# Two slices of an input weight loaded together, in 4,096-byte rows

## The chip, the cores and the metric

The kernel runs on one core of a Trainium2 chip. The metric is the device time of one execution in microseconds; the time of the kernel before is the median of three executions. Where the text works inside an execution, it uses one profiled execution, with times counted from the start of its span.

## What is computed

Cosformer attention (8 batches, 8 heads, 576 positions, 64 features a head) is followed by a two-layer feed-forward block with a swish whose slope is learned per hidden feature.

```python
# attention, q, k, v: (8, 8, 576, 64)
q_p, k_p = phi(q, cos_w, sin_w), phi(k, cos_w, sin_w)   # [relu(x)*cos, relu(x)*sin]
kv = np.einsum('bhsf,bhsd->bhfd', k_p, v)
z = np.sum(k_p, axis=2)
num = np.einsum('bhsf,bhfd->bhsd', q_p, kv)
den = np.einsum('bhsf,bhf->bhs', q_p, z)[..., None] + 1e-06
x = (num / den).transpose(0, 2, 1, 3).reshape(4608, 512)
# feed-forward, w_in: (512, 2048), w_out: (2048, 512), beta: (2048,)
h = x @ w_in
g = h * (1.0 / (1.0 + np.exp(-beta * h)))
out = g @ w_out
```

## The kernel before

The 4,608 tokens are nine chunks of 512. For each chunk TensorE computes h in 16 tiles of 128 hidden features (512 deep, so four matmuls a tile, numbered mi = 0 to 3), ScalarE applies Silu with beta as scale, and TensorE multiplies by w_out. Chunks 0 and 1 do this with plain matmuls (L384 for h; L542 for the output of chunk 0); the later ones use a Strassen-like scheme. Attention of batch b is woven in between, so that x of the next chunk is ready in time. The program order of each engine is the order in which the code is written: nothing reorders it, and an instruction that waits holds all behind it on its engine.

Both weights come from HBM in float32 and are cast to bfloat16 in SBUF. w_in is loaded in four slices of 512 of the 2,048 hidden features. Slice i goes into one staging buffer of 128 partitions x 4 x 512 float32 (there are four such buffers), one request for each mi, each of 128 rows of 2,048 bytes (L101). Because x comes transposed in an order of its own, partition 2d + jj of the buffer at place mi = 2 jp + g holds row 256 jp + 128 jj + 64 g + d of w_in; in HBM neighbouring rows lie 8,192 bytes apart. `cast_win` (L106) then writes `win[i]` in bfloat16. For slices 1, 2 and 3 this is `cast_halves` (L752): two casts on VectorE, each over all four mi and one half of the 512 columns. Slice i feeds h's tiles 4i to 4i + 3.

The four parts of w_out (`load_w("out", 0)` to `3`) take the same four staging buffers again, each as soon as the casts that read it are done.

All these loads are issued by SP's queue, in this order: q, v and k of batch 0, slice 0 of w_in (L135), slices 1 to 3 (L722), then in `rest()` w_out 0 and 1, then raw_v, raw_k and raw_q of batch 1 (L765 to L767, one 1,152 KB request each, recorded as L79), then w_out 2 and 3 in halves. Each request has one of eight completion semaphores, taken in turn, and SP waits before an issue until the request eight before it has landed.

VectorE's order around the change is: casts of slice 1; in `rest()` casts of slices 2 and 3; a division step for the last block of batch 0 (L306, L310, L317); eight casts of w_out (L122); the scaling of raw_v of batch 1 (L217); relu of raw_k (L191); relu of raw_q (L191).

TensorE's order is: h tiles 0 to 4 of chunk 0, a few matmuls of attention, then (`rest()` stands here) h tiles 5 to 15 without a break, then the output matmuls of chunk 0 (L542). Between these it does `kv_mm` of batch 1 (L274, needs the relu of raw_k) at place 22 of the loop over 32 places, and at place 23, in `second()`, the transposes of q of batch 1 (L233), which need the relu of raw_q.

Of the kernel before, what the change touches and what calls it, by code (L numbers as in the profile page):

```python
# [22 lines left out]
def kernel(  # L23
# [14 lines left out]
    nc = tc.nc  # L38
# [37 lines left out]
    def load_raw(b, name, j0=0, j1=4):  # L76
        js = slice(j0, j1)
        src = {"q": q, "k": k, "v": v}[name][b]
        nc.sync.dma_start(  # L79
            out=raw_tile(b, name)[:, js].rearrange("q j n d -> q j (n d)"),  # L80
            in_=src.rearrange("(j g) (p n) d -> (g p) j (n d)", g=2, n=NQ)[:, js, :])

    win = [const.tile([P, MI, 512], BF16, name=f"win{i}") for i in range(4)]
# [7 lines left out]
    w_in_v = moe_w_in.rearrange("(jp jj g d) f -> jp g d jj f", jp=2, jj=2, g=2)  # L91
    w_out_v = moe_w_out.rearrange("(j p) m -> p j m", p=P)
    stages = {}

    def load_w(kind, i, step=4):
        if (kind, i) not in stages:
            stages[kind, i] = stage.tile([P, 4, 512], FP32, name="w_stage", tag="w_stage")
        st = stages[kind, i]
        if kind == "in":
            for mi in range(MI):  # L100
                nc.sync.dma_start(out=st[:, mi], in_=w_in_v[mi // 2, mi % 2, :, :, i * 512 : (i + 1) * 512])  # L101
            return
        for a in range(0, 4, step):
            nc.sync.dma_start(out=st[:, a : a + step], in_=w_out_v[:, 4 * i + a : 4 * i + a + step, :])

    def cast_win(i, mis, eng="dve", f0=0, f1=512):  # L106

        o, a = win[i][:, mis, f0:f1], stages["in", i][:, mis, f0:f1]
        if eng == "act":
            nc.scalar.copy(o, a)  # L110
        elif eng == "pool":
            nc.gpsimd.tensor_copy(o, a)
        else:
            nc.vector.tensor_copy(o, a)

    def cast_out(j, eng="d"):
        i, jj = divmod(j, 4)
        st = stages["out", i]
        if eng == "a":
            nc.scalar.activation(wout[:, j, :], st[:, jj, :], AF.Copy, scale=rbeta[:, j : j + 1])  # L120
        else:
            nc.vector.tensor_scalar(wout[:, j, :], st[:, jj, :],  # L122
                                    scalar1=rbeta[:, j : j + 1], scalar2=None, op0=ALU.mult)
# [9 lines left out]
    load_raw(0, "k", 2, 3)  # L133
    load_raw(0, "k", 3, 4)
    load_w("in", 0, 2)  # L135


# [55 lines left out]
    def q_relu(b, jp, eng="dve", n0=0, n1=NQ):  # L193
        return relu(qb[:, jp, n0:n1].rearrange("q n (j d) -> q j n d", j=2),
                    raw_tile(b, "q")[:, 2 * jp : 2 * jp + 2, n0:n1], eng)

    def k_relu(b, j0=0, j1=4, eng="dve", n0=0, n1=NQ):
        relu(rk.rearrange("q n j d -> q j n d")[:, j0:j1, n0:n1], raw_tile(b, "k")[:, j0:j1, n0:n1], eng)

    def v_scale(b, cs, jp=None, n0=0, n1=NQ, eng="dve"):  # L200
        t = (cos9, sin9)[cs]
        rv = raw_tile(b, "v")
        js = slice(0, 4) if jp is None else slice(2 * jp, 2 * jp + 2)
        if jp is not None and eng != "act":
            if eng == "dve":
                t = ps[:, 0, 16 * cs : 16 * cs + NQ]
            (nc.gpsimd if eng == "pool" else nc.vector).tensor_tensor(
                vb[:, n0:n1, js, cs, 0:D],
                rv.rearrange("q j n d -> q n j d")[:, n0:n1, js],
                t[:, n0:n1].unsqueeze(2).unsqueeze(3).to_broadcast([P, n1 - n0, 2, D]), op=ALU.mult)  # L210
            return
        for n in range(n0, n1):
            o, a = vb[:, n, js, cs, 0:D], rv[:, js, n, :]
            if eng == "act":
                got = nc.scalar.activation(o, a, AF.Copy, scale=t[:, n : n + 1])  # L215
            else:
                got = nc.vector.tensor_scalar(o, a, scalar1=t[:, n : n + 1], scalar2=None, op0=ALU.mult)  # L217
        return got
# [82 lines left out]
    def x_rden(bank, slot, n0, n1, jps):  # L301

        w, m = len(jps), n1 - n0
        nv = ps[:, bank : bank + 2, slot * E : (slot + w * m) * E].rearrange("q j (i s e) -> q j i s e", s=w, e=E)
        den = small.tile([P, 2, m, w], FP32, name="den", tag=f"den{m}{w}")
        nc.vector.tensor_tensor(  # L306
            den, nv[:, :, :, :, D],
            eps9[:, n0:n1].unsqueeze(1).unsqueeze(3).to_broadcast([P, 2, m, w]), op=ALU.add)
        rden = small.tile([P, 2, m, w], FP32, name="rden", tag=f"rden{m}{w}")
        nc.vector.reciprocal(rden, den)  # L310
        return nv, rden, n0, jps

    def x_mul(got, n0, n1):
        nv, rden, first, jps = got
        a, z, w = n0 - first, n1 - first, len(jps)
        o = xs[:, n0:n1, jps[0] : jps[-1] + 1].rearrange("q n s (d j) -> q j n s d", j=2)
        nc.vector.tensor_tensor(  # L317
            o.rearrange("q j n s d -> q j (n s) d"),
            nv[:, :, a:z, :, 0:D].rearrange("q j n s d -> q j (n s) d"),
            rden[:, :, a:z].rearrange("q j n s -> q j (n s)").unsqueeze(3).to_broadcast([P, 2, (z - a) * w, D]),  # L320
            op=ALU.mult)
# [41 lines left out]
    def x_turn_dma(b, n0, n1):  # L363
        for c, o, n0, n1 in pieces(b, n0, n1):
            nc.sync.dma_start(out=xt_tile(c)[:, o : o + n1 - n0].rearrange("q n s c -> q (n s) c"),
                              in_=xs[:, n0:n1].rearrange("q n s c -> q (n s c)"), transpose=True)
# [354 lines left out]
    for i in range(1, 4):  # L721
        load_w("in", i)  # L722
# [17 lines left out]
    for mi, eng in enumerate(("pool", "dve", "act", "pool")):  # L740
        cast_win(0, slice(mi, mi + 1), eng)
# [10 lines left out]
    def cast_halves(i):  # L752
        for f in (0, 256):
            cast_win(i, slice(0, MI), "dve", f, f + 256)
# [2 lines left out]

    def rest():

        cast_halves(2)  # L760
        cast_halves(3)
        x_mul(x_rden(2, 0, 8, NQ, (0, 1)), 8, NQ)
        load_w("out", 0)
        load_w("out", 1)
        load_raw(1, "v")  # L765
        load_raw(1, "k")
        load_raw(1, "q")  # L767
        load_w("out", 2, 2)
        load_w("out", 3, 2)
        x_turn_dma(0, 8, 9)  # L770
        for j in range(8):
            cast_out(j)
        v_scale(1, 0)
        v_scale(1, 1, n0=8)
        k_relu(1, 0, 2)
        q_relu(1, 0)
        q_relu(1, 1, n1=5)
# [8 lines left out]
    def second():  # L786
# [14 lines left out]

    early = {
        4: lambda: (num_mm(0, 8, 0, 2, 0), num_mm(0, 8, 1, 2, 1), rest()),
        15: lambda: (v_scale(1, 1, n1=8, eng="act"), k_relu(1, 2, 4, "act")),
        22: lambda: (kv_mm(1, 0, 6), kv_mm(1, 1, 6), kv_take((0, 1), 6, "act"), q_relu(1, 1, "act", 5)),
# [281 lines left out]
```

## Time and profile before

| what | value |
|---|---|
| median of three executions | 276.92 us (275.34, 276.92, 278.1) |
| the profiled execution's own time | 277.77 us |
| its span in the profile | 275.6 us |
| TensorE matmuls (PE) busy | 265.4 us, 96% of the span |
| TensorE weight loads (PEld) busy | 206.8 us, 75% |
| VectorE (DVE) busy | 218.9 us, 79% |
| ScalarE (ACT) busy | 188.6 us, 68% |
| GpSimd (POOL) busy | 62.8 us, 23% |
| moved by the DMA engines | 54.00 MB in 50,856 packets |
| hardware queue of SP (q1) | 47,680 packets, 45.56 MB, 60.7% of 16 engines' span |
| w_in requests | 16 of 256 KB, 5.5 us from issue to landing (median) |
| w_out requests | 2 of 1,024 KB, 9.5 us, and 4 of 512 KB, 12.1 us |

Engines are named as in the profile: PE and PEld are TensorE's matmuls and weight loads, DVE is VectorE, ACT is ScalarE, POOL is GpSimd, SP issues most transfers; SPq is its queue. A line such as L384 is a line of the kernel and can be one in a helper. Idle time of an engine carries the name of what ended it. A request runs on all 16 DMA engines; each engine works its own share off in order and reports once, and the request has landed with the sixteenth report. Times of instructions come from one execution; matmuls are pipelined and their ends are modelled.

### The profile page before, as it was taken

What the parts mean: (1) busy time and instruction counts of PE and PEld (TensorE: products, weight loads), DVE (VectorE), ACT (ScalarE), POOL (GpSimd) and SP (SyncE); (2) the same over time, 40 slices, a digit from 0 to 9 for tenths busy, and PEclk for the clock granted to TensorE, in tenths of its full rate; (3) what the DMA queues carried; (4) which work ended last, traced back from release to release, by engine and by line L of the source; (5) the groups of instructions that cost most, each with busy time, mean ns of one, the idle gap of its engine ahead of it and who ended that gap; (6) DMA issues with size and microseconds to landing.
All of it is one profiled execution on the core that took longest, in us unless ns stands there. A gap on an engine that the chain in (4) does not pass through costs nothing.

```text
span 275.6 us, 8960 instructions
## 1 busy us (share of the span) xinstructions
PE 265.4 (96%) x3712; PEld 206.8 (75%) x3712; DVE 218.9 (79%) x581; ACT 188.6 (68%) x384; POOL 62.8 (23%) x82
## 2 busy tenths in 40 slices
PE   8789998999899999999999999999999999999994
PEld 8444445545784578888888888878888888888883
DVE  5875559499989989899988997898589868758852
ACT  5678778697418647799579966987696169428910
POOL 1320000330059100560075009400840060000000
PEclk9999999999999999999999999999999999999999
DMA  6999999999998998994499658973600560015005
GB/s 231 380 347 336 397 390 289 392 227 321 298 133 289 293 345 167 248 358 100 102 227 354 135 59 207 337 75 59 172 11 2 61 177 8 2 26 128 0 2 152
DMA packets 50856, 54.00 MB, mean 196 GB/s; under 512 B 31408, under 2 KB 31936, under 8 KB 50816
## 3 DMA queue, kind: packets, MB, share of 16 engines
q1 hardware_dynamic: 47680, 45.56, 60.7%
q0 software_dynamic: 2784, 7.61, 9.5%
q8 instruction: 29, 0.48, 0.8%
q10 hardware_dynamic: 352, 0.27, 0.4%
q14 instruction: 11, 0.09, 0.2%
HBM read 36.71 MB, written 9.44 MB: 167 GB/s over the span
## 4 chain that ended last, share of the span: by engine, by line
PE 86%; DMA 9%; DVE 1%; issue 1%; SPq 1%; ACT 0%
PE ps L619 31%; PE ps L509 27%; PE ps L384 12%; DMA raw_q<-in_q_dram 6%; PE ps L561 4%; PE ps L295 4%; DMA raw_v<-in_v_dram 4%; PE ps L274 3%; PE ps L542 3%; SPq L79 1%; PE ps L354 1%; PE ps L233 0%; DVE xs L317 0%; DVE qb L191 0%; DVE rden L310 0%
## 5 line engine op out<-in xcount | busy, mean ns | idle before, releaser
L535 POOL DMA_DIRECT2D out_dram<-o_sb x58 | 33.4, 582 | 157.9 <-ACT o_sb L656 87.2
L418 ACT ACTIVATE g_t<-ps,beta 128x512 bf16<-128x512 f32 x96 | 60.4, 704 | 1.4 <-PE ps L509 1.3
L619 PEld LDWEIGHTS <-S 128*128 128x128 bf16 x448 | 43.4, 98 | 5.2
L509 PE MATMUL ps<-w_stage 128*128 128x256 bf16 x288 | 46.6, 272 | 0.0
L384 PE MATMUL ps<-xt,win 128*128 128x512 bf16 (+1 forms) x196 | 42.8, 375 | 0.0
L509 PEld LDWEIGHTS <-w_stage 128*128 128x128 bf16 x384 | 37.3, 98 | 4.9
L392 ACT ACTIVATE g_t<-ps,beta 128x512 bf16<-128x512 f32 x48 | 32.3, 689 | 7.2 <-PE ps L384 7.1
L485 DVE TENSOR_TENSOR ps<-ps,p 128x256 f32<-128x256 f32 x74 | 30.5, 428 | 8.4 <-PE ps L509 2.9
L619 PEld LDWEIGHTS <-g_t 128*128 128x128 bf16 x336 | 32.3, 98 | 4.5 <-ACT g_t L418 0.4
L384 PEld LDWEIGHTS <-win 128*128 128x128 bf16 x196 | 18.7, 98 | 20.9
L509 PE MATMUL ps<-xt,win 128*128 128x256 bf16 x192 | 32.9, 272 | 0.0
L509 PEld LDWEIGHTS <-win 128*128 128x128 bf16 x288 | 28.0, 98 | 3.5
L619 PE MATMUL ps<-wout,g_t 128*128 128x256 bf16 x224 | 28.9, 273 | 0.0
L478 ACT COPY ps<-ps 128x256 f32<-128x256 f32 x62 | 22.6, 384 | 8.2 <-PE ps L619 4.8
L404 DVE TENSOR_TENSOR S<-g_t 128x512 bf16<-128x512 bf16 (+1 forms) x66 | 25.7, 419 | 3.0 <-ACT g_t L418 1.9
L215 ACT ACTIVATE vb<-raw_v,sin 128x256 bf16<-128x256 f32 (+1 forms) x58 | 26.1, 506 | 2.6 <-DMA raw_v<-in_v_dram 2.6
L619 PE MATMUL ps<-T,S 128*128 128x256 bf16 x224 | 26.6, 273 | 0.0
L619 PE MATMUL ps<-wout,S 128*128 128x256 bf16 x224 | 26.4, 273 | 0.0
L317 DVE TENSOR_TENSOR xs<-ps,rden 128x768 bf16<-128x768 f32 (+4 forms) x26 | 24.3, 941 | 0.9 <-DVE rden L310 0.2
L217 DVE TENSOR_SCALAR vb<-raw_v,cos 128x256 bf16<-128x256 f32 x63 | 19.9, 365 | 1.3 <-DMA raw_v<-in_v_dram 1.3
L221 POOL TENSOR_TENSOR qs<-qt,tanr 128x1152 bf16<-128x1152 bf16 x6 | 14.3, 2390 | 28.1 <-DMA qt<-qb 21.5
L656 ACT COPY o_sb<-ps 128x512 f32<-128x512 f32 x11 | 6.3, 587 | 20.1 <-PE ps L619 20.1
(112 smaller groups left out, 399.4 us busy)
## 6 DMA issues: line engine op xcount, KB each, us to landing
raw_v<-in_v_dram SPq DMA_DIRECT2D x7, 1152.0 KB, 10.3
raw_k<-in_k_dram SPq DMA_DIRECT2D x7, 1152.0 KB, 9.8
raw_q<-in_q_dram SPq DMA_DIRECT2D x7, 1152.0 KB, 7.5
out_dram<-o_sb POOLq DMA_DIRECT2D x58, 128.0 KB, 4.7
w_stage<-in_moe_w_in_dram SPq DMA_DIRECT2D x16, 256.0 KB, 5.5
w_stage<-in_moe_w_out_dram SPq DMA_DIRECT2D x2, 1024.0 KB, 9.5
w_stage<-in_moe_w_out_dram SPq DMA_DIRECT2D x4, 512.0 KB, 12.1
out_dram<-o_sb SPq DMA_DIRECT2D x10, 128.0 KB, 2.3
```

The costliest lines, as they stand in the source:

```text
L215: got = nc.scalar.activation(o, a, AF.Copy, scale=t[:, n : n + 1])
L217: got = nc.vector.tensor_scalar(o, a, scalar1=t[:, n : n + 1], scalar2=None, op0=ALU.mult)
L317: nc.vector.tensor_tensor(o.rearrange("q j n s d -> q j (n s) d"), nv[:, :, a:z, :, 0:D].rearrange("q j n s d -> q j (n s) d"), rden[:, :, ...
L384: nc.tensor.matmul(ps[:, h_bank(c, jt), i * 64 : (i + w) * 64], lhsT=win[jt // 4][:, mi, (jt % 4) * P : (jt % 4 + 1) * P], rhs=xt[:, i : i ...
L392: return nc.scalar.activation(gs[c, jt // 4][:, jt % 4], ps[:, h_bank(c, jt)], AF.Silu, scale=beta[:, jt : jt + 1])
L404: return nc.vector.tensor_tensor(o, l, r, op=op)
L418: return nc.scalar.activation(gs[c, jt // 4][:, jt % 4], bank, AF.Silu, scale=beta[:, jt : jt + 1])
L478: return nc.scalar.copy(at("a", 0), at("b", 0))
L485: nc.vector.tensor_tensor(dst, at("b", 0), st["p5"], op=ALU.add)
L509: nc.tensor.matmul(dst, lhsT=l[:, g], rhs=r[:, :, g * HP : (g + 1) * HP], start=start and g == 0, stop=g == 1, skip_group_check=True)
L535: (eng or own).dma_start(out=out_v[bb, n][:, m0:m1], in_=o_sb[hf * HP : (hf + 1) * HP, m0:m1])
L619: nc.tensor.matmul(dst, lhsT=l(i), rhs=r[:, i], start=start and i == 0, stop=i == order[-1], skip_group_check=True)
```

## The change

Slices 0 and 1 of w_in are loaded as before. Slices 2 and 3, which are columns 1,024 to 2,047, are loaded together: instead of four requests for each slice, one for each mi with rows of 2,048 bytes, there are four requests in all, one for each (jp, g), each of 128 rows of 4,096 bytes that span both slices. The staging buffer that held slice 2 now holds jp = 0 of both slices, and the one that held slice 3 holds jp = 1 of both. The casts of these slices are cut differently to match: each still covers 128 x 1,024 elements, but two mi and all 512 columns, in place of all four mi and 256 columns. So each slice needs both staging buffers. Their order is slice 2 jp 0, slice 2 jp 1, slice 3 jp 0, slice 3 jp 1.

```diff
@@ load_w
-        if kind == "in":
+        if kind == "in" and i < 2:
             for mi in range(MI):
                 nc.sync.dma_start(out=st[:, mi], in_=w_in_v[mi // 2, mi % 2, :, :, i * 512 : (i + 1) * 512])
             return
+        if kind == "in":
+            for g in range(2):
+                nc.sync.dma_start(out=st[:, 2 * g : 2 * g + 2].rearrange("q a f -> q (a f)"),
+                                  in_=w_in_v[i - 2, g, :, :, 1024:2048])
+            return
@@ cast_win
-        o, a = win[i][:, mis, f0:f1], stages["in", i][:, mis, f0:f1]
+        o = win[i][:, mis, f0:f1]
+        if i < 2:
+            a = stages["in", i][:, mis, f0:f1]
+        else:
+            a = stages["in", 2 + mis.start // 2].rearrange("q (g u) f -> q g u f", g=2)[:, :, i - 2, f0:f1]
@@ rest
-        cast_halves(2)
-        cast_halves(3)
+        for i in (2, 3):
+            for jp in range(2):
+                cast_win(i, slice(2 * jp, 2 * jp + 2))
```

## The prediction

> **What bounds the kernel now.** I read the page first, for the chain of work that ended last (shares of the span by engine).
>
> ```profile
> PE 86%; DMA 9%; DVE 1%; issue 1%; SPq 1%; ACT 0%
> ```
>
> TensorE sets the end, and transfers own a tenth of it. The chain in order of time (start, us, what), for 20 to 44 us, shows where that tenth touches this change:
>
> ```profile
> 23.36 2.30 PE ps L384 x11
> 25.65 15.69 DMA raw_q<-in_q_dram
> 41.35 0.03 issue
> 41.37 0.77 DVE qb L191
> 42.14 0.05 issue
> 42.19 1.18 PE ps L233 x18
> ```
>
> The reader is to see that TensorE's work at 42.19 us hangs on the landing of raw_q of batch 1, a transfer that stands behind all of w_in in SP's queue. Then the waits of PE (us in total, times, longest), for 12 to 60 us:
>
> ```profile
> PE ps L233 <- DVE qb L191: 0.7, 1, 0.7
> ...
> PE ps L274 <- DVE rk L191: 0.4, 2, 0.2
> ```
>
> and for 43 us to the end:
>
> ```profile
> PE ps L295 <- issue: 1.5, 2, 0.9
> ```
>
> So all that a faster queue can give TensorE is 0.70 us before L233 and, by the timeline of PE, 0.18 us before the L274 of batch 1 (39.18 us): 0.88 us. After 43 us no transfer and no engine holds TensorE, so what it gains or loses at 42.19 us reaches the end whole. Next the timeline of DVE, where the casts stand (start, us, idle before and its releaser):
>
> ```profile
> 22.98 1.29 DVE L114 CAST win<-w_stage 128x1024 bf16<-128x1024 f32 x2 [1.62 <-DMA w_stage<-in_moe_w_in_dram]
> 25.69 1.29 DVE L114 CAST win<-w_stage 128x1024 bf16<-128x1024 f32 x2 [1.41 <-DMA w_stage<-in_moe_w_in_dram]
> ...
> 29.68 1.68 DVE L122 TENSOR_SCALAR wout<-w_stage,rbeta 128x512 bf16<-128x512 f32 x4 [1.93 <-DMA w_stage<-in_moe_w_out_dram]
> ```
>
> The casts wait for transfers, not for DVE. Last, busy time by stretch (its last two figures are the DMA engines' share and GB/s) and SP's own timeline:
>
> ```profile
> 20.00:26.00 6.00, 6.00 (x49) 3.07 (x47) 2.90 (x5) 5.09 (x9) 0.00 (x0) 1.00 0.98 328
> 26.00:34.00 8.00, 8.00 (x39) 3.63 (x37) 5.02 (x13) 6.19 (x9) 0.00 (x0) 1.00 1.04 387
> 34.00:42.00 8.00, 7.31 (x100) 3.43 (x97) 4.11 (x13) 5.57 (x11) 0.00 (x0) 1.00 1.05 390
> ```
>
> ```profile
> 18.00 2.99 SPq L101 DMA_DIRECT2D w_stage<-in_moe_w_in_dram  x4
> 21.18 1.01 SPq L104 DMA_DIRECT2D w_stage<-in_moe_w_out_dram  x2
> 22.23 0.72 SPq L79 DMA_DIRECT2D raw_v<-in_v_dram  x1
> ```
>
> The DMA engines are saturated up to 42 us; the stretch with w_in moves 328 GB/s where the later ones move 390. A request counts as landed when the slowest of its 16 engines is done, and in the trace's landing events that engine trails the first by 1.4 to 2.9 us. Its work is what counts, and in these events it is busy nearly throughout: from the first request of slice 2 on, each 256 KB lands 0.65 us after the one before.
>
> **The change part by part.** *Rows.* Slices 2 and 3 are 8 requests of 128 rows of 2,048 bytes: 64 packets on each engine. They become 32 packets of 4,096. In the trace's packet records a 2,048-byte packet takes 84 ns (median), a 1,024-byte one 46, a 2,304-byte one 93; SP's queue has none of 4,096, but GpSimd's output queue does, at 159 ns. From 1,024 to 2,048 bytes costs 38 ns, so 4,096 would be 84 + 2 x 38 = 160 ns: both rows agree on 8 to 9 ns saved a pair, 32 x 8 = 0.26 us. The other end: by landing steps the 2,304-byte rows go at 94 ns a packet, 24.5 bytes/ns, against 81.5 ns (25.1 bytes/ns) for 2,048, so longer rows need not be better; at 24.5 bytes/ns 4,096 takes 167 ns against 163, a loss of 32 x 4 = 0.13 us. I take 0.26, since one of its rows has the very size.
>
> [...] The trace's rows decide for me: 256 bytes take 18 ns and 1,024 take 46, so 9 ns of every packet are fixed.
>
> *Fewer requests.* Four completion packets fewer on each engine, 9 ns each by the packet records: 0.04 us. Four issues fewer on SP, some 0.54 us each plus waits (the smallest and median of L101's durations are 534 and 536 ns). A request waits for the landing of the one eight before it, which is why SP sends one every 0.65 us from 13 to 20 us. With twice the bytes in a request, w_out's first request leaves at about 18.3 us (when the casts of slice 0 are done) instead of 21.18. That buys nothing on the slowest engine where it is not starved: w_out 0 was issued at 21.18 and landed at 29.65. What might be starvation: one step of 0.93 and one of 0.74 us among the 0.65s (0.37 over), and w_out 0 taking 4.08 us where w_out 1 takes 2.66; of those 1.42 us, 0.955 are one packet of queue 8, instruction loading, that begins at 25.10, which leaves 0.47 unexplained. Bounds 0 to 0.84; I take 0, because each of these requests had been issued 3 to 8 us before it landed.
>
> *Casts.* Four of 128x1024 before and after, at 694 and 685 ns; source and target keep two free dimensions, so 0 (10 ns either way). What changes is who needs what. Before, tile 8 of h (the first of slice 2) needed DVE's first cast of slice 2, ended at 23.68, and its matmuls began at 25.89. Now its third matmul needs the second cast, which waits for the last w_in request of all. That landed at 25.57 before; 0.12 to DVE's start and 0.69 for the cast give 26.38, and with the 98 ns weight load about 26.5, against 26.32 where that matmul began: a new wait of 0.2 us on TensorE if the queue gains nothing, none if it gains 0.2 or more. Behind it in TensorE's order stand all of h's tiles 9 to 15 and ScalarE's Silus. Its cover is the 0.88 us that TensorE waits later; without that it would cost its 0.2. Tiles 12 to 15 need slice 3's casts at 29.34; they end near 27, 2 us early. On DVE behind the casts stand 0.8 us of work at L306 to L317, and then 1.93 us idle, which hides a cast that ends 0.2 us later.
>
> *Staging buffers* come free after the third and fourth cast instead of the second and fourth: w_out 2 takes the first of them, and SP reached it at 28.98, over 2 us after that.
>
> *Sum.* The queue lands 0.26 + 0.04 = 0.30 us earlier from slice 3 on (bounds -0.13 and 0.29 + 0.04 + 0.84 = 1.17). raw_q lands at 41.05, TensorE's turn begins at 41.89, and the end moves by 0.30 us, as 0.30 is under 0.88 and over 0.2. What is late next is raw_q still.
>
> **The rivals.** *The whole wait goes (B).* If the 328 GB/s was starvation and 4 KB rows cure it, the queue gains about 1 us, and TensorE's 0.88 us close entirely: 276.0 us. For it: the low rate, and the long steps. Against it: the slowest engine's even 0.65 us steps. It can't give more, as TensorE has nothing else to win.
>
> *Hidden or not done (C).* The packets stay at the old bytes per ns, or are cut at 2,048 bytes again: gain 0 to 0.04 us, the new 0.2 us wait falls in the later one: 276.9.
>
> *Long rows are slow (D), the slower side.* The trace's longest packets do move worse: 8,192 bytes take 423 ns (median of 18), 16,384 take 1,085 (of 29), and of the 4,096-byte packets one in ten takes over 350. At 423/2 = 211 ns the 32 packets cost 32 x (211 - 163) = 1.5 us; slice 3, raw_q and the turn come 1.5 us later, and tile 8 waits inside that: 278.5. At 1,085/4 = 271 ns it is 3.5 us, 280.4. It is over 1% from 163 + 2,800/32 = 250 ns a packet on. Against it: those long packets are instruction and table loads on other queues, and the undisturbed 4,096-byte packet takes 159.
>
> **How the numbers follow.** The profiled execution took 277.77 us (span 275.6), 0.85 over the median 276.92; in it I expect 277.47, and as a median 276.92 - 0.30 = 276.6. Chances: forecast 0.50, B 0.17, C 0.15, D 0.18. One per cent is 2.8 us, and it is also the spread of the three runs (275.34 to 278.1), about what a measurement can tell from no change. None of the forecast, B and C leaves it by itself. With the spread of runs on top of B and the forecast I give faster 0.09; half of D's cases reach it with the spread: slower 0.10; within 0.81. Range: from 275.3 (B with the run spread) to 278.5 (D by the 8,192-byte row), with some 0.07 left out below and 0.10 above.
>
> **What would show it.** Right: the DMA packets of queue 1 fall by 512 data packets and 64 completions; the last w_in lands near 25.3, raw_q near 41.05; PE's wait before L274 at 39 us goes, the one before L233 shrinks from 0.70 to about 0.6 us (41.31 to 41.89), and none appears at L384. B: that wait is gone and the rate in 20 to 26 us is near 390. C: raw_q at 41.3 and some 0.2 us of wait at L384. D: casts of slice 2 in two halves far apart, a long wait at L384 near 26.3 us, and L233 after 43 us. The forecast is wrong if the end moves by other than raw_q's landing.

## The result and the profile after

Twenty runs of each kernel: 276.96 us before (median, 274.73 to 278.46), 275.55 us after (274.0 to 279.69). The ratio is 0.995 with a 95% interval of 0.9925 to 0.9974, a gain of 0.7 to 2.1 us. Two later comparisons with fresh runs gave 0.9964 [0.9931, 0.9997] and 0.9988 [0.9951, 1.0025]; the mean of the three, weighted by the inverse square of the intervals' widths, is 0.996 plus or minus 0.002, some 1.0 us (0.5 to 1.5). The profiled execution took 274.12 us with a span of 272.0, so it was 1.4 us under its median, as that of before was 0.8 us over its own: the 3.65 us between the two are not the change's effect alone. The profile of the first repetition, further down, is of a slow execution (278.23 us), and nothing rests on its times.

The page of the changed kernel, its chain by engine:

```profile
PE 89%; DMA 8%; issue 0%; DVE 0%; SPq 0%; DVEq 0%
```

The same chain in order of time, from 20 to 44 us:

```profile
16.12 8.56 DMA w_stage<-in_moe_w_in_dram
...
24.78 0.71 DVE win L123
25.49 0.05 issue
25.53 6.65 PE ps L393 x30
32.18 0.86 PE ps L551 x4
...
38.23 1.15 PE ps L283 x72
39.37 0.16 issue
39.53 0.81 PE ps L551 x3
40.34 1.00 PE ps L242 x18
```

Before, the chain ran through the landing of raw_q to the transposes of q (L233, now L242). Now it runs through the last w_in request and the second cast (L123) to TensorE's tile 8 (L393), and from there it is TensorE's work almost to the end. The waits of PE, 12 to 60 us, say the same: the one before the transposes is gone, a small one at L393 is new.

```profile
PE ps L304 <- ACT kv L293: 0.5, 1, 0.5
PE ps L393 <- DVE win L123: 0.3, 1, 0.3
PE ps L283 <- DVE rk L200: 0.2, 1, 0.2
PE ps L551 <- issue: 0.2, 1, 0.2
```

VectorE's timeline. The first cast stands alone, since the second needs the other staging buffer; w_out 0 (L131) is now there before VectorE asks:

```profile
22.22 0.69 DVE L123 CAST win<-w_stage 128x1024 bf16<-128x1024 f32 x1 [1.23 <-DMA w_stage<-in_moe_w_in_dram]
24.78 1.90 DVE L123 CAST win<-w_stage 128x1024 bf16<-128x1024 f32 x3 [1.87 <-DMA w_stage<-in_moe_w_in_dram]
...
27.42 1.68 DVE L131 TENSOR_SCALAR wout<-w_stage,rbeta 128x512 bf16<-128x512 f32 x4
```

And busy time by stretch, with the DMA engines' rate at the end:

```profile
20.00:26.00 6.00, 5.67 (x42) 2.35 (x41) 2.90 (x6) 4.97 (x8) 0.00 (x0) 1.00 1.03 401
26.00:34.00 8.00, 7.95 (x38) 3.64 (x38) 5.57 (x17) 6.31 (x10) 0.00 (x0) 1.00 1.05 390
```

401 GB/s from 20 to 26 us, where before it was 328. Queue 1 has 47,104 packets in place of 47,680, 576 fewer, as 512 data packets and 64 completions make. The trace's packet records give 159 ns (median) for the 512 packets of 4,096 bytes.

Not all of raw_q's lead belongs to the change. The profile of before ran late ahead of anything that was changed: its first w_in request landed at 15.37 us, in the changed kernel's at 14.06. So more profiles of both were needed, and the experiments gave them.

### The profile page after: what moved, and what is told of

It is laid out like the page before. It is cut to its first block, busy times and chain, and to the rows that moved or that the text cites. A ratio compares the mean times of both kernels' runs of the same rounds, so it can differ in the third digit from the quotient of the medians.

```text
span 272.0 us, 8950 instructions
## 1 busy us (share of the span) xinstructions
PE 264.6 (97%) x3708; PEld 206.7 (76%) x3712; DVE 218.2 (80%) x581; ACT 188.3 (69%) x384; POOL 62.8 (23%) x82
## 3 DMA queue, kind: packets, MB, share of 16 engines
q1 hardware_dynamic: 47104, 45.56, 60.7%
## 4 chain that ended last, share of the span: by engine, by line
PE 89%; DMA 8%; issue 0%; DVE 0%; SPq 0%; DVEq 0%
PE ps L628 32%; PE ps L518 27%; PE ps L393 13%; DMA w_stage<-in_moe_w_in_dram 6%; PE ps L551 5%; PE ps L570 5%; PE ps L304 4%; PE ps L283 3%; DMA raw_v<-in_v_dram 2%; PE ps L242 0%; SPq L79 0%; PE ps L363 0%; DVE win L123 0%; DVE o_sb L659 0%; DVEq L123 0%
## 5 line engine op out<-in xcount | busy, mean ns | idle before, releaser
L393 PE MATMUL ps<-xt,win 128*128 128x512 bf16 (+1 forms) x196 | 43.0, 375 | 0.4 <-DVE win L123 0.3
L393 PEld LDWEIGHTS <-win 128*128 128x128 bf16 x196 | 18.7, 98 | 21.6 <-DVE win L123 0.8
```

What stands on the lines that cost most here:

```text
L393: nc.tensor.matmul(ps[:, h_bank(c, jt), i * 64 : (i + w) * 64], lhsT=win[jt // 4][:, mi, (jt % 4) * P : (jt % 4 + 1) * P], rhs=xt[:, i : i ...
```

## The experiments

Two theories stood against each other. *Supply*: in the kernel before, the faster of the 16 DMA engines run out of work, as at most eight requests are in flight and each is small; larger requests cure it. *Rows*: longer rows do it. A third had to be excluded, that the first pair of profiles differed by chance.

**The kernel before once more.**

> The kernel before once more, for a second profile of it. All theories: 277.0 us within 0.3%. In the first profile the DMA engines moved 328 GB/s from 20 to 26 us and the first w_in request landed at 15.4 us; in the profile of the changed kernel it landed at 14.1 us, ahead of anything that the change touches. If that lead of 1.3 us is a difference between executions, this profile should show a landing somewhere between 13.5 and 15.5 us, and a wait of TensorE before the transposes of q (0.7 us in the first profile) that is not the same as there. The low rate from slice 1 of w_in on should be there again (320 to 350 GB/s) if it belongs to the kernel.

Ratio 0.9992 [0.9959, 1.0026]. Its second w_in request landed at 14.89 us, in the first profile at 16.04 and in the changed kernel's at 14.74, so the early lead is a difference between executions. The low rate and the wait are there again (stretch, then TensorE's timeline):

```profile
20.00:26.00 6.00, 6.00 (x45) 2.77 (x43) 1.99 (x4) 5.22 (x9) 0.00 (x0) 1.00 1.00 316
```

```profile
40.84 1.18 PE L233 MATMUL ps<-ident,qb 128*128 128x128 bf16 x18 [0.71 <-DVE qb L191]
```

**The changed kernel, twice more.**

> The changed kernel once more: ratio 0.995 within 0.003 (275.6 us). Supply theory (with at most eight requests in flight, requests of 256 KB leave the faster DMA engines without work, larger ones do not): the rate while slices 2 and 3 and w_out 0 move is 385 GB/s or more again, and TensorE does not wait before the transposes of q. If the first profile was a lucky execution: the rate is again near 330 and the wait is back.

> The changed kernel once more, beside the others of this call: ratio 0.995 to 0.9965; in the profile, turn of q between 39.9 and 41.2 us with no wait or a short one before it.

Ratios 0.9964 [0.9931, 0.9997] and 0.9988 [0.9951, 1.0025]. In the profile of the second repetition the rate from 20 to 26 us was 397 GB/s, and no wait stood before the transposes of q (waits of PE, 12 to 60 us):

```profile
PE ps L304 <- issue: 1.9, 1, 1.9
PE ps L304 <- ACT kv L293: 0.5, 1, 0.5
PE ps L393 <- DVE win L123: 0.2, 1, 0.2
```

The new wait at tile 8 was 0.2 us here. The first repetition's profile had 403 GB/s and no wait before the transposes either, but 1.47 us at tile 8. The reader also sees why one profile can't weigh a gain of 1 us: a single "issue" wait of TensorE, for which the profile shows no releaser, took 1.9 us here and 0.5 in the first profile of the changed kernel.

**Rows alone, first try.** Rows of 4,096 bytes, eight requests of 256 KB, each of 64 neighbouring partitions:

```diff
-                nc.sync.dma_start(out=st[:, 2 * g : 2 * g + 2].rearrange("q a f -> q (a f)"),
-                                  in_=w_in_v[i - 2, g, :, :, 1024:2048])
+                for u in range(2):
+                    nc.sync.dma_start(out=st[u * 64 : (u + 1) * 64, 2 * g : 2 * g + 2].rearrange("q a f -> q (a f)"),
+                                      in_=w_in_v[i - 2, g, u * 32 : (u + 1) * 32, :, 1024:2048])
```

> The changed kernel with its four 512 KB requests cut into eight of 256 KB, each 64 partitions of 4,096-byte rows: the rows of the change with the request count and bytes in flight of before. Row theory (longer rows move faster): like the changed kernel, 275.6 us, rate 385 GB/s or more. Supply theory: like the kernel before, 277.0 us, rate about 330 while slices 2 and 3 move, and SP again waits for a landing before each of these requests.

Neither: 282.67 us, ratio 1.0209 [1.0162, 1.0257]. The 4,096-byte packets took 256 to 270 ns from 19 to 24 us (means by the us), where the change's took 160 to 162, and the rate fell to 255 GB/s. TensorE's timeline, 20 to 32 us, shows where that went:

```profile
22.14 1.04 PE L394 MATMUL ps<-xt,win 128*128 128x512 bf16 x4 [0.64 <-DVE win L124]
...
30.59 1.80 PE L394 MATMUL ps<-xt,win 128*128 128x512 bf16 x5 [3.96 <-DVE win L124]
```

The run says nothing on rows; it shows that requests for 64 neighbouring partitions were slow here. No run shows why.

**Rows alone, second try.** The same eight requests, but each for every second partition:

```diff
-                nc.sync.dma_start(out=st[:, 2 * g : 2 * g + 2].rearrange("q a f -> q (a f)"),
-                                  in_=w_in_v[i - 2, g, :, :, 1024:2048])
+                for jj in range(2):
+                    nc.sync.dma_start(out=st[jj::2, 2 * g : 2 * g + 2].rearrange("q a f -> q (a f)"),
+                                      in_=w_in_v[i - 2, g, :, jj, 1024:2048])
```

> The changed kernel with eight requests of 256 KB in place of four of 512, rows still 4,096 bytes, each request for every second partition so that it covers both halves of the partitions (the run with 64 neighbouring partitions had packets of 256 ns). Descriptor theory (before, DMA engines wait for descriptors once their backlog is used up, some 150 to 165 rows a us over all engines; a longer row brings more bytes with each): like the changed kernel, ratio 0.995 to 0.998, 4,096-byte packets at 160 ns mean, 385 GB/s or more from 20 to 26 us, no wait before the transposes of q. Request theory (the number of requests is what counts): like the kernel before, ratio 1.000, rate 320 to 340. If it is again the half of the partitions that a request covers: packets well over 160 ns and over 1.01.

Ratio 1.001 [0.997, 1.005], the request theory's number. But the profile is half way: 358 GB/s from 20 to 26 us (packets of 160 to 188 ns, means by the us from 19 to 23 us), and no wait before the transposes of q, only 0.31 us at tile 8.

```profile
20.00:26.00 6.00, 5.69 (x43) 2.51 (x42) 2.10 (x4) 5.06 (x8) 0.00 (x0) 1.00 1.00 358
```

**Requests alone, twice.** The kernel before with two mi in one request, rows of 2,048 bytes, casts as before (added lines only):

```diff
@@ load_w
+        if kind == "in" and i >= 2:
+            for jp in range(2):
+                nc.sync.dma_start(out=st[:, 2 * jp : 2 * jp + 2],
+                                  in_=w_in_v[jp, :, :, :, i * 512 : (i + 1) * 512].rearrange("g d jj f -> d jj g f"))
+            return
```

> The kernel before with slices 2 and 3 loaded in two requests of 512 KB each, still in rows of 2,048 bytes (two mi in one request), casts as before. Supply theory: like the changed kernel or better, 275.3 to 275.6 us, rate 385 GB/s or more, and no wait at the first tile of slice 2, since its cast needs no later slice. Row theory: like the kernel before, 277.0 us, rate about 330.

> Rows of 2,048 bytes in requests of 512 KB once more, beside the change: in the first comparison it was 0.9993 [0.9965, 1.0021] while the change was 0.9964. If requests alone do it: 0.996. If both longer rows and larger requests are needed: 0.999 to 1.000, with a wait before the transposes of q of 0.7 us again and a low rate (under 350 GB/s) from 16 us until the w_in packets are gone.

Ratios 0.9993 [0.9965, 1.0021] and 1.000 [0.9967, 1.0034]: no gain. From 16 to 20 us the rate was 300 and 315 GB/s, from 20 to 26 us 354 and 334. TensorE's timeline of the first, 36 to 43 us, has both late waits:

```profile
39.18 1.33 PE L279 MATMUL ps<-vb,rk 64*64 64x130 bf16 x72 [1.03 <-DVE rk L196]
40.43 1.04 PE L547 MATMUL ps<-wout,g_t 128*128 128x512 bf16 x4
42.18 1.01 PE L238 MATMUL ps<-ident,qb 128*128 128x128 bf16 x15 [0.71 <-DVE qb L196]
```

**Half the row length.** If the DMA engines waited for row descriptors, rows of 1,024 bytes would be a disaster. Eight requests of 256 KB with 256 rows each (of the added lines, those that differ from the edit above):

```diff
@@ load_w
+            for jp in range(2):
+                for f in (0, 256):
+                    nc.sync.dma_start(out=st[:, 2 * jp : 2 * jp + 2, f : f + 256],
+                                      in_=w_in_v[jp, :, :, :, i * 512 + f : i * 512 + f + 256].rearrange("g d jj f -> d jj g f"))
```

> The kernel before with slices 2 and 3 in eight requests of 256 KB whose rows are 1,024 bytes (two mi and half the columns in one request), so the same requests and bytes with twice the rows. Descriptor theory: at 150 to 200 rows a us these 2,048 rows take 10 to 13 us in place of some 5.6, the rate there falls to 160 to 200 GB/s, TensorE waits 4 us or more at h tiles 8 to 12, and the time is 280 to 284 us, ratio 1.013 to 1.03. Packet theory (each packet has a fixed cost of 9 ns and nothing else): 128 packets of 46 ns in place of 64 of 84, 0.5 us later, ratio 1.000 to 1.003.

Ratio 1.0006 [0.9969, 1.0042]; the descriptor theory falls. The engines took 324 to 346 of these packets a us from 18 to 22 us, about twice what that theory allowed, at 342 to 356 GB/s. The rate from 20 to 26 us is even above the 328 and 316 of the kernel before, and the time is no better:

```profile
20.00:26.00 6.00, 6.00 (x45) 2.72 (x43) 2.46 (x4) 5.24 (x9) 0.00 (x0) 1.00 1.07 358
```

**The cut of the casts alone.** The diff is the change's last hunk.

> The kernel before with only the cut of the casts changed (two mi and all 512 columns in one cast, loads as before). All theories: the casts take 0.69 us as before and the first tile of slice 2 needs both casts, which end near 24.3 us, 2 us before that tile; ratio 1.000 within 0.003. If it came out below 0.997, the cut of the casts would have a part in the gain.

Ratio 1.0015 [0.9979, 1.0051]: no part in the gain. Its profile had the wait before the transposes (0.44 us) and another one behind it, at L542 for a cast of w_out:

```profile
40.25 1.18 PE L233 MATMUL ps<-ident,qb 128*128 128x128 bf16 x18 [0.44 <-DVE qb L191]
...
42.07 1.89 PE L542 MATMUL ps<-wout,g_t 128*128 128x512 bf16 x8 [0.64 <-DVE wout L122]
```

**Is raw_q what sets TensorE's turn?** The changed kernel with 1 MB of unneeded loads ahead of raw_q:

```diff
         load_raw(1, "k")
+        for t, j in ((T1, 0), (T2, 2)):
+            nc.sync.dma_start(out=t.rearrange("q i t -> q (i t)").bitcast(FP32).rearrange("q (j m) -> q j m", j=2),
+                              in_=w_out_v[:, j : j + 2, :])
         load_raw(1, "q")
```

> The changed kernel with 1 MB of loads that nobody needs put ahead of raw_q of batch 1 (2.7 us of the queue at 390 GB/s; w_out 2 and 3 come later by as much). Theory that the landing of raw_q sets TensorE's turn and that nothing after it gives time back: TensorE waits some 2.5 us before the transposes of q, they begin near 42.6 us instead of 39.9 to 41.2, and the time grows by 2.4 to 2.8 us over the change: ratio to the kernel before 1.004 to 1.007. If TensorE had slack there, less: 0.996.

Ratio 1.0083 [1.0049, 1.0117], 278.56 us, and the wait is back (TensorE's timeline):

```profile
42.99 1.28 PE L242 MATMUL ps<-ident,qb 128*128 128x128 bf16 x18 [2.48 <-DVE qb L200]
```

Against the change's 0.996 that is about 3.4 us (2.3 to 4.4 by the two intervals), against the changed kernel's median in the same comparison (275.54 us) 3.0. The wait of 2.48 us is not given back. That the loss is more than the wait lies within the interval; a reason for more, a granted clock of 0.50 for 3.4 us, is told in the last section.

**What can a faster queue give at most?** The kernel before without the loads of slice 3:

```diff
@@ load_w
+        if (kind, i) == ("in", 3):
+            return
@@ cast_win
-        o, a = win[i][:, mis, f0:f1], stages["in", i][:, mis, f0:f1]
+        o, a = win[i][:, mis, f0:f1], stages["in", min(i, 2)][:, mis, f0:f1]
```

> The kernel before without the loads of slice 3 of w_in (its casts read slice 2's staging buffer, so the output is not the reference's): everything behind it in SP's queue lands some 2.6 us earlier. It shows what a faster queue could give at most here. Theory: raw_q is there before TensorE asks, no wait at L233 and none at tile 8, and TensorE gains the whole of its later waits, 0.7 to 0.9 us and no more: ratio 0.995 to 0.9975, the same as the change's. If the queue holds TensorE elsewhere too: 0.990 or less.

Ratio 0.9953 [0.9921, 0.9984], with no wait at tile 8 nor before the transposes. TensorE was busy without a break from 20 to 42 us; the last stretch of that, where the kernel before has 7.31 us in 8.00:

```profile
34.00:42.00 8.00, 8.00 (x119) 4.55 (x117) 4.96 (x13) 5.66 (x12) 0.00 (x0) 1.00 1.05 386
```

So leaving a whole megabyte out gains 1.3 us (0.4 to 2.2), about as much as the change does: with raw_q there in time, TensorE has no wait for it left to lose. The queue itself gained less than the 2.6 us expected: relu of raw_q began at 39.39 us, where the two profiles of the kernel before have 41.37 and 40.03.

**Taking the new wait away.** The change with the 128 columns of tile 8 cast first:

```diff
-        for i in (2, 3):
-            for jp in range(2):
-                cast_win(i, slice(2 * jp, 2 * jp + 2))
+        cast_win(2, slice(0, 2))
+        for f0, f1 in ((0, 128), (128, 512)):
+            cast_win(2, slice(2, 4), "dve", f0, f1)
+        for jp in range(2):
+            cast_win(3, slice(2 * jp, 2 * jp + 2))
```

> The changed kernel with the cast of slice 2, jp 1, cut once more, so that the 128 columns of the first tile are cast first (256 elements a partition, some 0.27 us in place of 0.69). In two profiles of the changed kernel TensorE waited 0.3 and 1.5 us at L393 for that cast. Theory that this new wait now sets the end: TensorE starts that tile 0.4 us earlier wherever it waits, ratio to the kernel before 0.993 to 0.996, a little under the change's 0.995 to 0.996. If the wait is covered later: same as the change.

Ratio 0.9959 [0.9925, 0.9994]. TensorE ran through tile 8 without a wait and began the transposes at 39.90 us without one:

```profile
22.84 4.48 PE L393 MATMUL ps<-xt,win 128*128 128x512 bf16 x20
```

The wait is gone, but the intervals can't tell this kernel from the change.

## Why the prediction was right in direction and too small in size

*What bounds the kernel: right.* All five profiles with the loads of before or with larger requests or shorter rows have 0.70 to 0.71 us of wait before the transposes of q, the one with only the casts cut has 0.44; the change's, the split casts, the ceiling and the second try with rows have none. The cap of 0.88 us, worked out from one profile, holds within the ceiling's interval. It is one execution's: the second profile of the kernel before has no wait for raw_k at 38 us and so 0.71 in all, while three variants waited 0.32, 0.41 and 1.03 us for raw_k alone. And "after 43 us no transfer holds TensorE" was true of that execution, but the cast kernel's waited 0.64 us for w_out at 42 us.

*Rows: the packet right, the saving too large.* 160 ns forecast, 159 measured. But what counts by the prediction's own words is the engine that lands last. There a 512 KB request landed 1.28 us after the one before (20.84, 22.12 in the landing events) where two of 256 KB took 1.31. That is 0.03 us a request and some 0.13 for all four, completions included, where the forecast had 0.30. The prediction's landing steps, 163 ns for a pair of packets against 160, had pointed to the smaller saving; it went by the packets' medians. By those (2 x 84 - 159 = 9 ns a pair) the 32 pairs would save an estimated 0.29 us, over twice what the landing steps show with the completions.

*Starvation: the term that was mis-sized.* The prediction took 0 between bounds of 0 and 0.84 us, "because each of these requests had been issued 3 to 8 us before it landed". The profiles speak for more. raw_q's relu starts at 41.37, 40.03 and 39.44 us (before, before again, casts alone), and at 39.14, 39.31 and 39.08 (change, change again, split casts). The means are 1.1 us apart, where the forecast had 0.30. Half of that was there ahead of anything that was changed: the second w_in request landed at 16.04, 14.89 and 14.69 us, and at 14.74, 14.56 and 14.69. Counted from there, raw_q's relu comes 25.33, 25.14 and 24.75 us later with the loads of before and 24.40, 24.75 and 24.39 with the change's: 0.56 us apart in the mean. With 0.13 for rows and completions, some 0.4 us are left for what the prediction put at nothing. Values of one kernel differ by as much, so the size is rough, and that it was starvation isn't shown. The rate doesn't show it: from 20 to 26 us it is 328, 316 and 339 GB/s with the loads of before and 401, 397 and 395 with the change's, but it is a mean over 16 engines, and rows of 1,024 bytes, at 358 GB/s, needed 25.48 us to the relu.

So the two terms missed in opposite directions, and the sum was still too small. Rival B, the whole wait closed, for 276.0 us or 0.9968, was nearer to the measured 0.996 than the forecast's 276.6 or 0.9988, and the signs that the prediction named for it are those seen: the wait gone and a rate near 390. By the waits in the profiles the change gives TensorE about 0.5 us (0.88 and 0.71 lost before, 0.33 and 0.19 after), the lower end of what the times say.

*The new wait: right in place.* 0.33, 0.19 and, in the kernel with rows alone, 0.31 us. The prediction had it vanish once the queue gained 0.2 us; that set the queue's gain against TensorE's timing in one execution. There the matmul in question began at 26.32 us; TensorE was ready for it at 25.20 and 25.55 in the two profiles of the change. What the wait costs isn't shown: with the casts split the transposes began at 39.90 us, where those profiles have 40.18 and 40.38, but the times can't tell the kernels apart.

*Casts and no give-back: right*, by the run with casts alone and the delay. The staging buffers held nothing up in the profile, though with less to spare: SP reached w_out 2 at 26.38 us, not 28.98.

*Rival D* did not happen to the change, but the first try with rows shows it: packets of 256 ns, past the 250 ns set as its 1% point, and a time 2.1% longer. It cost 6.4 us where the prediction's price at that point was 2.8: TensorE waited 4.6 us in all at tiles 4 and 8, and then ran at a granted clock of 0.50 for 3.4 us, as the last section shows. The packets of 8,192 and 16,384 bytes that the prediction set aside are those of queues 14 and 8; the records call both instruction, and table loads aren't shown.

*What stays open* is which half of the change does it, and why. Larger requests alone gain nothing (two intervals around 1.000). Longer rows alone remove the wait in their profile, at 358 GB/s, and raw_q's relu comes 24.57 us after the second w_in landing, as in the changed kernel; with larger requests alone it came 26.21 and 25.45 us after. That speaks for the rows. Yet the times of rows alone are 1.001 [0.997, 1.005]; this interval and the change's 0.996 plus or minus 0.002 overlap a little, so that both halves are needed isn't shown either. The descriptor theory fell with the short rows, and larger requests alone contradict the supply theory. The cause of the low rate in 16 to 28 us isn't settled.

## What to carry to other kernels

Read a load's price from the first instruction that waits at the end of its queue, not from the load's own consumer: here w_in's packets were paid 15 us later, at raw_q. Before hoping for more from a faster queue, measure the ceiling by leaving a transfer out; here one such kernel gained 0.5% (0.2 to 0.8), about what the change gave. And don't cut a load into requests for 64 neighbouring partitions unmeasured: the one try here took 2.1% longer.

## What the runs showed of the hardware

*The last report trails the other fifteen.* A landing is the sixteenth report: before, raw_q's came at 41.35 us, and its relu began at 41.37. The first w_in request had its fifteenth report at 14.26 us and its sixteenth at 15.37, 1.11 us later; at the last w_in request it was 0.05 us (25.52, 25.57), at raw_q 0.63 (40.72, 41.35). Packets of queue 8 (16,384 bytes of instructions; 0.91, 0.94 and 0.96 us at 9.9, 19.0 and 25.1 us there) are of the size of the longest of these lags, and raw_q's relu, which waits for the sixteenth report, began anywhere between 39.4 and 41.4 us in three profiles with the loads of before. Which DMA engine carries them isn't in the records, so this is a reading, not shown.

*A request for 64 neighbouring partitions* ran its 4,096-byte packets at 256 to 270 ns (means by the us, 19 to 24 us), one for every second partition at 160 to 197 and one for all at 160 to 171 (from 18 us on).

*TensorE's granted clock fell to 0.50 after waits of 1.91, 2.48 and 3.96 us.* In the run with the delay TensorE waited 2.48 us until 42.99. Its busy time by stretch (the third figure from the end is the granted clock):

```profile
40.00:44.00 4.00, 1.52 (x21) 1.03 (x20) 1.65 (x4) 1.39 (x3) 0.00 (x0) 0.99 1.05 387
44.00:47.00 3.00, 3.00 (x11) 1.12 (x9) 3.00 (x5) 2.51 (x6) 0.00 (x0) 0.50 1.14 288
47.00:50.00 3.00, 3.00 (x120) 1.59 (x119) 1.76 (x5) 2.39 (x4) 0.00 (x0) 0.94 0.98 342
```

The clock's records have 0.50 from 43.94 to 47.35 us. From these 3.41 us at 0.50, an estimate of what they cost beyond the wait itself is up to 1.7 us. In the first try with rows the clock was 0.50 from 31.16 to 34.57 us, after a wait of 3.96 us; by the same estimate that adds up to 1.7 us to the 4.6 us waited. In the second repetition of the changed kernel it was 0.50 from 47.36 to 50.77 us, after the "issue" wait of 1.91 us. Waits of 0.7 and 1.03 us, and one of 1.52 in the kernel without slice 3, left it at 1.00. So in these runs gaps of 1.91, 2.48 and 3.96 us were each followed by 3.41 us at 0.50, and by the estimate above the price of such a wait is more than its length.
